# A sparse attention and gated feed-forward kernel: the first K through two cast loads, the row table early, one pair of the second chunk scored ahead

## The chip, the cores and the metric

The kernel runs on one core of a Trainium2 chip. A core has TensorE (PE: matmuls and their weight loads, PEld), VectorE (DVE), ScalarE (ACT), GpSimd (POOL) and SyncE (SP), each with its own queue of instructions that it works off in order, and 16 DMA engines that all queues share. DMAs are issued by SP, ACT and POOL; only those of POOL change the type on the way (a "cast load": float32 in memory, float16 in SBUF). The metric is the device time of the kernel in microseconds, the median of several runs. Matmul results land in PSUM, which has 8 banks.

## The reference

Block-sparse attention over 4 batches, 8 heads, 768 positions, head size 64, followed by a gated feed-forward layer on 3072 tokens:

```python
scores = (1/8) * q @ k^T                       # per batch and head, 768 x 768
mask = neighbours | first/last block row or column | sampled_blocks   # 32 x 32 blocks
attn = softmax(where(mask, scores, -1e9));  o = attn @ v
x = o transposed to (batch*seq, 512)
out = (sigmoid(x @ w_gate) * (x @ w_val)) @ w_out      # 512 -> 1536 -> 512, float32 out
```

The mask is the same for all batches and heads; three sampled blocks per block row come in as a table of 64-bit integers.

## The kernel before

The work is cut into 12 **chunks** n of 256 queries (three per batch) and, in each, 4 **pairs** p of heads. `attend(n, p, seq)` handles one pair of one chunk: three score tiles (TensorE, two banks each, L628), three exponentials on ScalarE (L646), values with the sum of the weights as a 65th column (L669), reciprocal and scaling on VectorE (L677, L680), and a transpose into x. For n = 0 the mask is added as a bias by extra matmuls in the scores (row table `e24`, called e in the trace, times `bias`); for every other chunk the exponentials are multiplied by a mask tile on VectorE (L654). Those nine mask tiles are made by `build_mask` (spread on TensorE L590, scaling on VectorE L598), and the bias by `expand` (L566, L575).

`ffn(g, seq)` handles the feed-forward of one chunk: 24 gate operations of 4 matmuls (L731, wg and wv in turn), a tanh on ScalarE (L750), a product on VectorE (L757), and 12 output operations of 2 matmuls (L775), then a scaling (L792) and a store.

Loads: the q, k and v of batch 0 come by POOL's cast loads (`load_half`, L429, in the order of FIRST); of pair 0, the first two sixths of q and k and the rest come apart. wg and wv (two halves each, L511) and w_out (three parts, L520) follow in the same queue. Later batches come as float32 by SP (`load`, L386), are cast by VectorE or ScalarE (`cast_qk`, `cast_v`) and, for q and k, transposed by DMA (`turn_dma`, L464). The q and k of batch 0 are transposed on TensorE (`turn_pe`, L447, copied out by L453).

The order is not written by hand. Each operation is handed to a `Plan` with an engine, an assumed duration, what it reads and writes, and a priority `prio` (lower is first). `Plan.run` plays a clock forward: whenever an engine is free it takes the operation of best priority whose inputs are there by the plan's own reckoning. The sequence that comes out is what each engine then executes in order. For loads the plan reckons a landing: a constant from LAND for the first ones, else a start after the issue (3.2 us for POOL, 1.9 for others), a shared DMA clock and `slack`. Operations `behind` others are only ordered after them. A value that is planned too early makes an engine wait in the program; it changes no result. While TensorE has nothing to do before 22 us of the plan, small matmuls on a zero tile (L370) are put in.

Rings hold the buffers: `pt` (exponentials, 12 tiles), x per pair and h per f (2 each). x limits how far attention runs ahead: the values of chunk n stand behind the last gate of chunk n - 2 (L834). From pair number CHAIN = 18 on, counted in order of scoring, a fixed sequence takes over TensorE: ROUND = "SoVgggoo", which is one pair's scores, an output operation, the values of the pair before, three times two gate operations, two output operations. Gates lag GLAG = 5 pairs behind and outputs OLAG = 9.

At the start, SP issues the small table mi, then q_in (early part of q, float32), k_in (later part of k, float32) and one half of e (L354); ACT issues the sampled blocks, ident, and the other half of e; POOL issues k_a (early part of k, cast), and then the list FIRST. ScalarE casts q_in (L483) and k_in (L484, giving k_b).

Of the kernel before, what the change touches and what calls it, by code (L numbers as in the profile page):

```python
# [9 lines left out]
f16 = mybir.dt.float16  # L10
f32 = mybir.dt.float32
# [4 lines left out]
B, H, S, D = 4, 8, 768, 64  # L16
BLK = 32
NB = S // BLK
NJ = S // 128
NP = H // 2  # L20
NCH = 3
CH = 256
# [5 lines left out]
VW = 66  # L28
SPIN = 22.0
NMASK = 1  # L30
FETCH = ((6, 1), (1, 2))
CHAIN, GLAG, OLAG, ROUND = 18, 5, 9, "SoVgggoo"
EDGES = [0, 768, 1536]
LAND = dict(sbi=2.9, mi=2.4, ident=3.1, e0=3.6, e1=3.9, q=2.9, kb=3.8, k=3.6)
FIRST = [
    ("k", 1), ("q", 1), ("k", 2), ("q", 2), ("v", 0), ("q", 0), ("k", 3), ("q", 3), ("v", 1), ("v", 2), ("v", 3),
]
HALF = [(0, 0), (0, 1), (0, 2), (0, 3)]
TURN_PE = 3
CAST_LATE = 12  # L40
GROUPS = [[i] for i in range(12)]
# [29 lines left out]
class Plan:  # L71
# [36 lines left out]
    def run(self):  # L108
# [10 lines left out]
        dma_free, mode, order, now = 0.0, None, [], 0.0  # L119
# [48 lines left out]
        while left:  # L168
            wake = []
            for e in LAT:  # L170
# [45 lines left out]
                o, where = best  # L216
# [7 lines left out]
                o.start, o.end = now, now + dur  # L224
                if o.lands is not None:
                    o.seen = o.lands
                elif o.dma:
                    first = now + (3.2 if e == "POOL" else 1.9)
                    if o.dma > 0.15:
                        first = dma_free = max(dma_free, first) + o.dma  # L230
                    o.seen = first + 0.3 + o.slack
                else:
                    o.seen = o.end + LAT[e]
# [13 lines left out]
            now = min(ahead)  # L247
# [13 lines left out]
def kernel(  # L261
# [11 lines left out]
    nc = tc.nc  # L273
# [40 lines left out]
    def psb(shape, dt=f32, homes=SINGLE, span=1):  # L314
        def make(i):
            t = psum[:, i : i + span].rearrange("p b c -> p (b c)")
            if dt != f32:
                t = t.bitcast(dt)
            n = int(np.prod(shape))
            t = t[:, 0:n]  # L320
            if len(shape) == 2:
                t = t.rearrange("p (a b) -> p a b", a=shape[0])
            return t

        b = Buf("ps", make)
        b.homes, b.span = homes, span
        return b

    def one(shape, dt, name):
        b = Buf(None, None)  # L330
        b.tile = sing.tile(shape, dt, name=name)
        return b
# [87 lines left out]
    def load_half(nm, b, p, prio, dur=0.72):  # L420
        cut = (nm, b, p) == ("q", 0, 0)
        js = later if cut else every
        if cut:
            c = one([128, 2, NJ - 2, 64], f16, "q16_late")
        else:
            c = sb(f"{nm}16" if nm != "v" else "vh", [128, 2, NJ, 64], f16)
        half16[nm, b, p] = stage[nm, b, p] = c
        o = P.op(
            "POOL", dur, lambda: nc.gpsimd.dma_start(c(), src[nm][b][:, 2 * p : 2 * p + 2, js]),  # L429
            writes=[c], prio=prio, dma=0.8 if cut else 1.0,  # L430
        )
        o.slack = 0.3 + b
        return o

    def turn_pe(nm, b, p, js, prio, behind=(), c=None, j0=0):
# [22 lines left out]
    def turn_dma(nm, b, p, prio):  # L458
# [6 lines left out]
            reads=[c], writes=[t], prio=prio, dma=1.3,  # L465
        )

    k_in, q_in = one([128, 2, NJ - 2, 64], f32, "k_in"), one([128, 2, 2, 64], f32, "q_in")
    k_a, k_b = one([128, 2, 2, 64], f16, "k16_a"), one([128, 2, NJ - 2, 64], f16, "k16_b")
    q_a = one([128, 2, 2, 64], f16, "q16_a")  # L470
    P.op(
# [1 line left out]
        lands=LAND["q"],  # L473
    )
    P.op(
        "SP", 0.5, lambda: nc.sync.dma_start(k_in(), src["k"][0][:, 0:2, later]), writes=[k_in], prio=-94, dma=1.0,
        lands=LAND["kb"],
    )
    P.op(
        "POOL", 0.82, lambda: nc.gpsimd.dma_start(k_a(), src["k"][0][:, 0:2, early]), writes=[k_a], prio=-95,  # L480
        dma=0.5, lands=LAND["k"],
    )
    P.op("ACT", 0.35, lambda: nc.scalar.copy(q_a(), q_in()), reads=[q_in], writes=[q_a], prio=-88)  # L483
# [100 lines left out]
    def build_mask(c, prio, behind):  # L584
# [21 lines left out]

    group_of = {n: (g, i) for g, ns in enumerate(GROUPS) for i, n in enumerate(ns)}
    xT = {
        (g, p): sb(f"x{p}", [128, 512], f16) for g in range(len(GROUPS)) for p in range(NP)
    }  # L610

    valued, scored = {}, []
# [1 line left out]
    def attend(n, p, seq):  # L614
# [3 lines left out]
        for tt in range(NCH):  # L618
# [25 lines left out]
            P.op(  # L644
                "ACT", 0.915,
                lambda st=st, pt=pt: nc.scalar.activation(  # L646
# [72 lines left out]
    def ffn(g, seq):  # L719
# [4 lines left out]
        for f in range(NF):  # L724
            both = psb([512])
            pair = [(both, 0), (both, 256)]
            for k, ((t, z), (nm, wt)) in enumerate(zip(pair, (("g", wg), ("v", wv)))):
# [15 lines left out]
                        behind=gates[-1:],  # L743
                    )
                )
            tg, h_ = sb("tg", [128, 512], f32), sb(f"h{f}", [128, 512], f16)
            hts[g, f] = h_
            P.op(
                "ACT", 0.17 + 0.43 * k_,
# [49 lines left out]
                )  # L799

    seq, turned, late_loads = 0, [], []
    for n in range(B * NCH):
        b, c = divmod(n, NCH)
        if n == 1:
            for p in range(NP):
                turn_pe("q", 0, p, later, 9.0, [valued[0, 1]], j0=2 if p == 0 else 0)
            expand(2, 4, 2, scored[1:2])
            build_mask(1, 11.5, scored[4:5])
            build_mask(2, 14.5, [valued[0, 2]])
            build_mask(0, 26, [valued[0, 3]])  # L810
        for p in range(NP):
            attend(n, p, seq)
            seq += 3
        if b + 1 < B:
            for p in range(NP) if c == 0 else ():
                if (b + 1, p) in HALF:
                    for nm in "kq":
                        turn_pe(nm, b + 1, p, every, 3 * NP * (3 * b + 2))
                    cast_v(b + 1, p, 3 * NP * (3 * b + 2))
                    continue  # L820
# [67 lines left out]
```

## Time and profile before

| | us |
|---|---|
| median of 6 runs | 292.85 (292.19 to 293.37) |
| the profiled execution | 292.73 |
| span from its first to its last instruction | 290.8 |
| TensorE busy in the span | 284.7 |
| ScalarE busy | 206.9 |
| VectorE busy | 196.3 |

Busy times are unions of the instructions' spans; matmuls are pipelined, so TensorE's busy time is not the time that its array computes. "Idle before" names what an engine waited for. TensorE's clock was granted in full all through. The DMA engines are loaded from 2 us to about 40 us, which is batch 0 and the weights, and less afterwards.

### The profile page before, as it was taken

To read this page: it belongs to the slowest core of one execution; us is meant where nothing else is said; L and a number is where in the kernel's file an instruction comes from. 1 tells how busy PE (TensorE), PEld (TensorE's weight loads), DVE (VectorE), ACT (ScalarE), POOL (GpSimd) and SP (SyncE) were. 2 spreads that over 40 slices of the span, in tenths; PEclk is the share of its full clock that TensorE was granted. 3 is DMA by queue.
4 is the path that set the end of the run, shared out by engine and by line. 5 is a ranking of instruction groups with operands and counts; after the bars stand their busy time and mean duration, and the time that the engine had idled before them with its cause. 6 is when DMAs were issued, how large, how long until landed. Compare 5 with 4: busy or idle time off the path is not lost.

```text
span 290.8 us, 8127 instructions
## 1 busy us (share of the span) xinstructions
PE 284.7 (98%) x3417; PEld 210.8 (72%) x3417; DVE 196.3 (67%) x458; ACT 206.9 (71%) x321; POOL 14.1 (5%) x23
## 2 busy tenths in 40 slices
PE   7999999999999999999999999999999999999995
PEld 6686766885786877777767767767777777777763
DVE  3479878997897577657867877756765765763230
ACT  3875589787988677678678678768768777772331
POOL 8730000000000000000000000000000000000000
PEclk9999999999999999999999999999999999999999
DMA  7999997991796873115477564011011020121003
GB/s 139 192 209 211 207 283 205 278 239 37 232 233 198 124 198 82 20 47 188 94 222 207 117 211 100 19 47 47 10 55 35 21 58 15 43 56 42 8 34 109
DMA packets 50788, 35.43 MB, mean 122 GB/s; under 512 B 31376, under 2 KB 47808, under 8 KB 50752
## 3 DMA queue, kind: packets, MB, share of 16 engines
q1 hardware_dynamic: 43576, 27.97, 36.9%
q0 software_dynamic: 6960, 6.88, 14.4%
q8 instruction: 26, 0.43, 0.7%
q14 instruction: 10, 0.08, 0.1%
q10 hardware_dynamic: 216, 0.07, 0.1%
HBM read 28.42 MB, written 6.29 MB: 119 GB/s over the span
## 4 chain that ended last, share of the span: by engine, by line
PE 90%; DMA 5%; POOL 3%; issue 1%; ACT 0%; POOLq 0%
PE psum L731 44%; PE psum L775 23%; PE psum L669 12%; PE psum L628 12%; DMA wv<-in_moe_w_val_dram 5%; POOL vh L429 1%; POOL q L429 1%; POOL k L429 1%; PE psum L590 0%; PE psum L705 0%; POOL k_a L480 0%; POOL wg L511 0%; POOL q_late L429 0%; ACT y L792 0%; POOLq L872 0%
## 5 line engine op out<-in xcount | busy, mean ns | idle before, releaser
L646 ACT ACTIVATE pt<-psum 128x1024 f16<-128x1024 f32 x144 | 138.9, 1026 | 23.6 <-PE psum L628 23.4
L654 DVE TENSOR_TENSOR pt<-pt,mask 128x1024 f16<-128x1024 f16 x132 | 89.3, 687 | 46.0 <-ACT pt L646 45.9
L731 PE MATMUL psum<-x,wv 128*128 128x256 f16 x576 | 86.5, 273 | 0.5 <-DMA wv<-in_moe_w_val_dram 0.5
L731 PE MATMUL psum<-x,wg 128*128 128x256 f16 x576 | 86.4, 272 | 0.0
L750 ACT ACTIVATE tg<-psum 128x256 f32<-128x256 f32 x144 | 56.0, 389 | 41.9 <-PE psum L731 40.0
L775 PE MATMUL psum<-wo,h 128*128 128x512 f16 (+1 forms) x300 | 75.4, 372 | 0.0
L757 DVE SCALAR_TENSOR_TENSOR h<-tg,psum 128x256 f16<-128x256 f32 x144 | 58.1, 416 | 24.1 <-ACT tg L750 23.5
L731 PEld LDWEIGHTS <-wv 128*128 128x128 f16 x576 | 55.4, 98 | 8.7 <-issue 1.7
L731 PEld LDWEIGHTS <-wg 128*128 128x128 f16 x576 | 53.5, 98 | 7.8 <-issue 1.3
L669 PEld LDWEIGHTS <-pt 128*128 128x128 f16 x1152 | 42.4, 97 | 9.6 <-issue 0.8
L628 PE MATMUL psum<-qT,kT 64*128 64x256 f16 x576 | 44.7, 271 | 0.0
L669 PE MATMUL psum<-v,pt 128*128 128x65 f16 x1152 | 44.3, 193 | 0.0
L775 PEld LDWEIGHTS <-h 128*128 128x128 f16 x300 | 26.1, 98 | 22.8 <-issue 7.6
L628 PEld LDWEIGHTS <-kT 64*128 64x128 f16 x576 | 24.4, 94 | 19.5 <-issue 16.7
L792 ACT ACTIVATE y<-psum 128x512 f32<-128x512 f32 (+1 forms) x22 | 12.7, 577 | 12.3 <-PE psum L775 12.3
L680 DVE TENSOR_TENSOR x<-psum,rz 128x256 f16<-128x256 f32 x48 | 20.3, 424 | 1.6
L677 DVE RECIPROCAL rz<-psum 128x4 f32<-128x4 f32 x48 | 8.6, 179 | 5.3 <-PE psum L669 5.1
L370 PE MATMUL psum<-zero 128*64 128x128 f16 x47 | 5.5, 277 | 1.0 <-DVE zero L340 1.0
L598 DVE TENSOR_SCALAR mask<-psum 128x512 f16<-128x512 f32 x9 | 6.1, 683 | 0.2
L628 PE MATMUL psum<-bias,e 64*128 64x256 f16 x48 | 5.8, 273 | 0.0
L406 DVE CAST v<-vs 128x768 f16<-128x768 f32 x10 | 5.5, 553 | 0.0
L370 PEld LDWEIGHTS <-zero 128*64 128x64 f16 x47 | 4.5, 147 | 1.4 <-DVE zero L340 1.0
(53 smaller groups left out, 69.9 us busy)
## 6 DMA issues: line engine op xcount, KB each, us to landing
out_dram<-y SPq DMA_DIRECT2D x23, 256.0 KB, 2.8
ks<-in_k_dram SPq DMA_DIRECT2D x12, 384.0 KB, 3.4
qs<-in_q_dram SPq DMA_DIRECT2D x12, 384.0 KB, 4.0
vs<-in_v_dram SPq DMA_DIRECT2D x12, 384.0 KB, 4.6
wg<-in_moe_w_gate_dram POOLq DMA_DIRECT2D x2, 768.0 KB, 13.5
wv<-in_moe_w_val_dram POOLq DMA_DIRECT2D x2, 768.0 KB, 16.4
wo<-in_moe_w_out_dram POOLq DMA_DIRECT2D x3, 512.0 KB, 21.8
vh<-in_v_dram POOLq DMA_DIRECT2D x4, 192.0 KB, 7.8
```

What stands on the lines that cost most here:

```text
L370: "PE", dur, lambda: nc.tensor.matmul(t()[0:64], zero()[:, 0:64], zero(), start=True, stop=True),
L429: "POOL", dur, lambda: nc.gpsimd.dma_start(c(), src[nm][b][:, 2 * p : 2 * p + 2, js]),
L628: nc.tensor.matmul(st()[:, hd, jj * CH : (jj + 1) * CH], l[r, 2 * tt + jj, :], m[r, 2 * c : 2 * c + 2, :], start=not (own and masked), sto ...
L646: lambda st=st, pt=pt: nc.scalar.activation(pt().rearrange("p h j q -> p h (j q)"), st(), AF.Exp, scale=SCALE),
L654: nc.vector.tensor_tensor(t, t, mask()[:, c, tt].unsqueeze(1).to_broadcast([128, 2, 512]), op=ALU.mult)
L669: nc.tensor.matmul(o()[:, 2 * jq + hd, 0:65], pts[j // 2]()[:, hd, j % 2, jq * 128 : jq * 128 + 128], v_[:, hd, j, 0:65], start=(j == 0), ...
L680: lambda: nc.vector.tensor_tensor(x16().rearrange("p j (h d) -> p (j h) d", d=64), o()[:, :, 0:64], rz().to_broadcast([128, 4, 64]), op=AL ...
L731: nc.tensor.matmul(t()[:, z : z + w], wt()[:, i, f * 128 : (f + 1) * 128], xT[g, i]()[:, 0:w], start=(i == 0), stop=(i == NP - 1),)
L750: lambda tg=tg, a=pair[0]: nc.scalar.activation(tg()[:, 0:w], a[0]()[:, a[1] : a[1] + w], AF.Tanh, scale=0.5),
L757: lambda tg=tg, a=pair[1], h_=h_: nc.vector.scalar_tensor_tensor(h_()[:, 0:w], tg()[:, 0:w], 1.0, a[0]()[:, a[1] : a[1] + w], op0=ALU.add, ...
L775: nc.tensor.matmul(py()[:, m], hts[g, f]()[:, tt * 128 : (tt + 1) * 128], wo()[:, f, m], start=(f == 0), stop=(f == NF - 1),)
L792: lambda py=py, y=y, m=m: nc.scalar.activation(y()[:, m], py()[:, m], AF.Copy, scale=0.5),
```

## The change

1. **First K.** k_in, its SP load and its ScalarE cast go. The later part of k of pair 0 comes as a second cast load on POOL, straight into k_b, right behind k_a.
2. **Row table early.** With k_in gone, SP issues its half of e right after q_in; on ACT, ident moves behind the other half of e (prio -98 to -92).
3. **Order of loads.** In FIRST, the later part of q of pair 0 moves from the sixth place to the first.
4. **Order of scoring.** EARLY = (0,0), (1,0), (0,1), (0,2), (0,3), then the rest as before. The transposes of the later part of q of pair 0, the second bias and masks 1 and 2 are ordered behind the first three score tiles, with new priorities; the other q transposes and mask 0 come when (1, 1) is reached. The rule that asks for two free double banks (`paired`) is left off for EARLY.
5. **Rings.** pt 12 to 15; x 2 to 4 (values of chunk n behind the gates of chunk n - 4); x, h and tg tiles are 256 wide instead of 512. CHAIN 18 to 16.
6. **The plan's reckoning.** New LAND constants; POOL loads start 2.5 us after issue instead of 3.2; slack of batch 0 0.3 to 0.4, of later batches 1.5 to 3.0, which orders the casts of these loads later; first loads on POOL count in the DMA clock.

```diff
+Q0P, M1P, M2P = -39.2, 14, 17
+XR, HR = 4, 2
+EARLY = [(0, 0), (1, 0), (0, 1), (0, 2), (0, 3)]
-CHAIN, GLAG, OLAG, ROUND = 18, 5, 9, "SoVgggoo"
+CHAIN, GLAG, OLAG, ROUND = 16, 5, 9, "SoVgggoo"
-LAND = dict(sbi=2.9, mi=2.4, ident=3.1, e0=3.6, e1=3.9, q=2.9, kb=3.8, k=3.6)
+LAND = dict(sbi=1.7, mi=1.6, ident=3.2, e0=3.4, e1=3.3, q=3.1, kb=4.4, k=3.5)
 FIRST = [
-    ("k", 1), ("q", 1), ("k", 2), ("q", 2), ("v", 0), ("q", 0), ("k", 3), ("q", 3), ("v", 1), ("v", 2), ("v", 3),
+    ("q", 0), ("k", 1), ("q", 1), ("k", 2), ("q", 2), ("v", 0), ("k", 3), ("q", 3), ("v", 1), ("v", 2), ("v", 3),
 ]
...
+                    dma_free = max(dma_free, o.lands - 0.3) if e == "POOL" else dma_free
-                    first = now + (3.2 if e == "POOL" else 1.9)
+                    first = now + (2.5 if e == "POOL" else 1.9)
...
-        ("v16", 8), ("vh", 4), ("pt", 12), ("rz", 2), ("x16", 4), ("tg", 2), ("y", 3),
+        ("v16", 8), ("vh", 4), ("pt", 15), ("rz", 2), ("x16", 4), ("tg", 2), ("y", 3),
...
-        P.ring(f"x{p}", 2)
+        P.ring(f"x{p}", XR)
-        P.ring(f"h{f}", 2)
+        P.ring(f"h{f}", HR)
...
-        "ACT", 0.4, lambda: nc.scalar.dma_start(ident16(), id_h.ap()), writes=[ident16], prio=-98, dma=0.1,
+        "ACT", 0.4, lambda: nc.scalar.dma_start(ident16(), id_h.ap()), writes=[ident16], prio=-92, dma=0.1,
...
-        o.slack = 0.3 + b
+        o.slack = 0.4 + 0.6 * b
...
-        "SP", 0.5, lambda: nc.sync.dma_start(k_in(), src["k"][0][:, 0:2, later]), writes=[k_in], prio=-94, dma=1.0,
+        "POOL", 0.72, lambda: nc.gpsimd.dma_start(k_b(), src["k"][0][:, 0:2, later]), writes=[k_b], prio=-94,
+        dma=0.8, lands=LAND["kb"],
-    P.op("ACT", 0.56, lambda: nc.scalar.copy(k_b(), k_in()), reads=[k_in], writes=[k_b], prio=-67)
...
-            o.paired, o.twin = not masked and 4 * n + p < CHAIN, psb([2, 512], homes=PAIR, span=2)
+            o.paired, o.twin = (n, p) not in EARLY and 4 * n + p < CHAIN, psb([2, 512], homes=PAIR, span=2)
...
+    order = EARLY + [i for i in order if i not in EARLY]
-        if n == 1:
+        if (n, p) == EARLY[1]:
+            turn_pe("q", 0, 0, later, Q0P, scored[:1], j0=2)
+            expand(2, 4, 2, scored[1:2])
+            build_mask(2, M2P, build_mask(1, M1P, scored[2:3]))
+        if (n, p) == (1, 1):
+            for i in range(1, NP):
+                turn_pe("q", 0, i, later, 9.0, [valued[0, 1]])
+            build_mask(0, 26, [valued[0, 3]])
-            for p in range(NP):
-                turn_pe("q", 0, p, later, 9.0, [valued[0, 1]], j0=2 if p == 0 else 0)
-            expand(2, 4, 2, scored[1:2])
-            build_mask(1, 11.5, scored[4:5])
-            build_mask(2, 14.5, [valued[0, 2]])
-            build_mask(0, 26, [valued[0, 3]])
...
-                    o.slack = 1.5
+                    o.slack = 3.0
...
-        g = group_of[n][0] - 2
+        g = group_of[n][0] - XR
```

More of the change, by code (lines that the diff above doesn't have):

```diff
@@ L466, in turn_dma @@
         )
-    k_in, q_in = one([128, 2, NJ - 2, 64], f32, "k_in"), one([128, 2, 2, 64], f32, "q_in")
+    q_in = one([128, 2, 2, 64], f32, "q_in")
     k_a, k_b = one([128, 2, 2, 64], f16, "k16_a"), one([128, 2, NJ - 2, 64], f16, "k16_b")
@@ L475 @@
     P.op(
[L476 to L479, printed above, removed]
         "POOL", 0.82, lambda: nc.gpsimd.dma_start(k_a(), src["k"][0][:, 0:2, early]), writes=[k_a], prio=-95,
@@ L482 @@
     )
+    P.op(
+        "POOL", 0.72, lambda: nc.gpsimd.dma_start(k_b(), src["k"][0][:, 0:2, later]), writes=[k_b], prio=-94,
+        dma=0.8, lands=LAND["kb"],
+    )
     P.op("ACT", 0.35, lambda: nc.scalar.copy(q_a(), q_in()), reads=[q_in], writes=[q_a], prio=-88)
-    P.op("ACT", 0.56, lambda: nc.scalar.copy(k_b(), k_in()), reads=[k_in], writes=[k_b], prio=-67)
     for i, (nm, p) in enumerate(FIRST):
@@ L608 @@
     xT = {
-        (g, p): sb(f"x{p}", [128, 512], f16) for g in range(len(GROUPS)) for p in range(NP)
+        (g, p): sb(f"x{p}", [128, CH * len(ns)], f16) for g, ns in enumerate(GROUPS) for p in range(NP)
     }
@@ L745, in ffn @@
                 )
-            tg, h_ = sb("tg", [128, 512], f32), sb(f"h{f}", [128, 512], f16)
+            tg, h_ = sb("tg", [128, w], f32), sb(f"h{f}", [128, w], f16)
             hts[g, f] = h_
@@ L801 @@
     seq, turned, late_loads = 0, [], []
-    for n in range(B * NCH):
+    order = [(n, p) for n in range(B * NCH) for p in range(NP)]
+    order = EARLY + [i for i in order if i not in EARLY]
+    for n, p in order:
         b, c = divmod(n, NCH)
-        if n == 1:
-            for p in range(NP):
-                turn_pe("q", 0, p, later, 9.0, [valued[0, 1]], j0=2 if p == 0 else 0)
-            expand(2, 4, 2, scored[1:2])
-            build_mask(1, 11.5, scored[4:5])
-            build_mask(2, 14.5, [valued[0, 2]])
-            build_mask(0, 26, [valued[0, 3]])
-        for p in range(NP):
[L812 to L820, printed above, removed]
+        if (n, p) == EARLY[1]:
[6 more added lines that the diff above has]
+            build_mask(0, 26, [valued[0, 3]])
+        attend(n, p, seq)
+        seq += 3
+        if p == NP - 1 and b + 1 < B and c == 0:
+            for p in range(NP):
                 for nm in "kqv":
```

## The prediction

> **What bounds the kernel now.** I read the page's busy shares first, then the chain of work that ended last, in order of time. In the page:
>
> ```profile
> PE 284.7 (98%) x3417; PEld 210.8 (72%) x3417; DVE 196.3 (67%) x458; ACT 206.9 (71%) x321; POOL 14.1 (5%) x23
> ```
>
> TensorE is the bound, and the chain shows how it runs once it is full:
>
> ```profile
> 103.47 2.62 PE psum L731 x24
> 106.09 0.86 PE psum L775 x4
> 106.95 0.76 PE psum L628 x12
> 108.25 0.76 PE psum L669 x24
> 109.01 2.62 PE psum L731 x24
> ```
>
> One round (24 gate matmuls, 6 output matmuls, one pair's scores and values) takes 109.01 - 103.47 = 5.54 us, without a stall, and repeats to 261 us. None of that work is touched. So the change can only win TensorE time lost in the filling, before both halves of wg and wv have landed. The second wv is issued at 13.13 and needs 19.3 us (its tile's view): 32.4 us. The timeline of that stretch:
>
> ```profile
> 1.80 0.46 SPq L476 DMA_DIRECT2D k_in<-in_k_dram  x1
> ...
> 2.30 0.43 SPq L354 DMA_DIRECT2D e<-bb_e  x1
> ...
> 6.10 0.30 PE L566 MATMUL psum<-e,mb 128*64 128x256 f16 x2 [0.89 <-DMA e<-bb_e]
> ...
> 6.92 0.28 PE L628 MATMUL psum<-bias,e 64*128 64x256 f16 x2
> ...
> 7.57 2.85 ACT L646 ACTIVATE pt<-psum 128x1024 f16<-128x1024 f32 x3 [1.89 <-PE psum L628]
> ...
> 24.92 0.61 PE L731 MATMUL psum<-x,wv 128*128 128x256 f16 x4 [0.49 <-DMA wv<-in_moe_w_val_dram]
> ```
>
> The first score waits for the bias, the bias for the table e, and e's SP half is issued behind the 256 KB of k_in. All else follows from that first exponential. The same stretch in windows, columns PE, PEld, DVE, ACT and POOL busy, clock, DMA share, GB/s:
>
> ```profile
> 7.57:20.70 13.13, 12.73 (x258) 9.64 (x258) 7.25 (x21) 11.53 (x12) 7.58 (x11) 1.00 1.25 200
> 20.70:24.92 4.22, 3.73 (x55) 2.43 (x52) 3.98 (x11) 1.95 (x2) 0.00 (x0) 1.00 1.16 209
> 24.92:32.40 7.48, 7.48 (x84) 5.43 (x84) 6.79 (x15) 4.64 (x9) 0.00 (x0) 1.00 1.17 209
> ```
>
> To 20.70, ACT is the feeder: 12 exponentials (the four pairs of chunk 0) in 13.13 us, 1.60 idle. VectorE is idle for 13.13 - 7.25 = 5.9 us there and then full (3.98 of 4.22, 6.79 of 7.48), because all nine mask tiles (L598, 683 ns each) are built only then. In 20.70 to 24.92 ACT manages 2 exponentials. That imbalance is what the change works on.
>
> How much has TensorE lost there? Between its first score (6.92) and 32.4 lie 25.5 us. Useful at their own pitch: 12 masked score tiles x 0.43, 5 plain x 0.22, 5 value groups x 0.79, 80 transposes x 0.03, 10 of x x 0.055, 8 mask spreads x 0.24, 11 gates x 0.44: 19.8. So 5.7 us is loss, and some 2.5 of it (a dozen changes between scores and full matmuls, each an "issue" gap of 0.21 on PEld) stays. The ceiling is about 3.2 us plus what an earlier start gives.
>
> **The change, part by part.**
>
> *K by two cast loads, e earlier.* Removed: SP's k_in (256 KB) and ACT's cast of it (0.62 us at 5.07). Added: one POOL issue of 128 KB, 0.72 us by the L429 rows, second in POOL's queue. e's SP issue moves from 2.30 to 1.80, its ACT issue from 1.80 to 1.37; ident goes behind it, 1.37 to 1.80, and at its 2.3 us lands at 4.1, under the q_a cast that ends at 4.32: no cost. With nothing large in front, e should land like the neighbouring small loads (ident 2.3 us, q_in 2.7 us after issue): 4.1 to 4.5, not 6.07. From e's landing to the first score took 6.92 - 6.07 = 0.85; but VectorE must then also copy the first kT and qT (0.29 each), which before were done ahead of the bias. k_a lands at 1.23 + 3.2 = 4.43, transposes and copies to 5.3. I take the first score at 5.6 (5.2 to 6.3): **1.3 us earlier**, and ACT with it (6.25).
>
> Is k_b in time for the second score tile? Here a rule speaks against the change: the Trainium skill, DMA: Bandwidth & Descriptors, sections Specifications and Issuing engine by pattern, calls the sync/scalar path generally faster, with a first byte after about 0.6 us against 1 us from GpSimd. The rows: k_in on SP took 3.2 us for 256 KB; k_a on POOL took 3.2 us for 64 KB; the POOL load now in k_b's place, k of pair 1 (192 KB), took 4.9. By the page's difference alone k_b would land 0.4 later than its bytes ask, about 1.80 + 3.2 + 0.25 + 0.4 = 5.6 (estimate); by the row of the same place 2.05 + 4.9 = 6.95, less about 0.3 for 64 KB fewer, 6.6. Without k_in in the engines beside it I take 5.4. k_in plus its cast was ready at 5.69, so at 5.4 nothing is lost, and at 6.6 the second exponential starts at 7.9 instead of 7.2: 0.7 of the 1.3 gone, still no loss against 8.5 before.
>
> *Queue positions.* Every later POOL load is issued 0.72 us later, and q_late moves ahead of k of pair 1. POOL waits for landings from 9.5 on (for k of pair 2, then q of pair 2) and wg is issued at 10.49 but lands at 21.2, so issue is not what limits; bytes are. The same skill page (Queues, rings and completion order) says each DMA engine takes turns between its queues packet by packet: bytes moved from SP's queue to POOL's then cost the weights nothing. The rows allow a little: the DMA share is 0.87 and 1.12 in 2:4 and 4:6 against 1.28 after, so bytes moved out of the early stretch may not find their place; 128 KB at 200 GB/s is 0.65 at most. I take weights 0.2 later; TensorE has attention meanwhile, so 0.1 on the end. q of pair 1 lands some 0.5 later than 7.95, but is now wanted only after the six tiles of pair 0, near 11: hidden.
>
> *Chunk 1 of pair 0 scored second.* Its transposes (8), VectorE copy (0.42), three plain tiles and values come forward, needing only q_late (about 6.2). It fills ACT while pairs 1 and 2 land: the 1.60 idle goes. 1.3 + 1.6 = 2.9 us of ACT, three exponentials at 0.95: all of (1, 0) is through by 20.7. Masks 1 and 2 are built from the third score on, six in the 5.9 us that VectorE has idle (6 x 0.69 = 4.1).
> TensorE work pulled ahead of 20.7: three tiles x 0.25 + values 0.79 + six spreads x 0.24 = **3.0 us**.
>
> *Refill.* That work is then missing between 20.7 and 32.4. Gates can't replace it (f 6 to 11 need the halves landing at 28.6 and 32.4). Further tiles can: VectorE, freed of six masks (4.1 us), can take 4.1 / 0.98 = 4 tiles more (0.69 multiply, 0.29 share of normalising), ACT too (6.6 of 11.7 busy). They bring 4 x 0.51 = 2.0, plus 0.25 of mode change each where they come singly. I count 2.2 of the 3.0 kept.
>
> *Rings (pt 15, x 4) and CHAIN 16.* pt lets a fifth pair be in flight, which (1, 0) needs; x 4 lets chunk 2's values go before group 0's gates; half-width tiles move nothing. Part of the refill, no extra. Two more rounds in the written order: TensorE has no gap in the chain from 83 to 95, and its rounds there, less regular, are no slower than 5.54 by more than the 0.2 of one mode change: 0.5 either way, I take 0.
> *Later casts ordered later* (slack 1.5 to 3.0): the page has no wait of DVE or ACT on a batch load, so nothing to win; batch 1's kT is issued at 45.87 and wanted near 60 (the 30 exponentials before 50.0 are all of batch 0, which has 36), so 1.5 us later is hidden; without that cover it costs 1.5.
>
> **Sum** against the profiled execution's 292.73 (span 290.8 + 1.9 around it): 2.2 - 0.1 = 2.1 less, 290.6; it stands 0.12 under the median 292.85, so **290.7**.
>
> **The rivals.**
> *More is won* (refill complete, chunk 1 fed without gaps): the ceiling, 3.2 + 0.4: about 289.2. For it: VectorE and ACT have the room. Against: singly scored tiles cost a mode change each.
> *Spent again*: the early work is done, and TensorE then waits at 24.9 and 32.4 for weights, which the change doesn't hasten: 292.5. For it: the wait at 24.92. Against: attention tiles are ready for such holes.
> *Slower: the order written for TensorE puts a transpose ahead of ready scores while its load is still out.* The plan now assumes POOL loads 0.7 us sooner after issue (2.5 for 3.2), with only 0.1 more slack in batch 0. Before, one such place cost 0.65 (PEld for q of pair 3 at 14.59). Behind it stand all scores, and ACT behind these. If seven K/Q loads each held it 0.6, that is 4.2, against 2.9 of ACT time won: 1.3 lost, 294.0. It decides from 0.4 us per load upwards; below that the two or three tiles waiting in PSUM hide it.
>
> **How the numbers follow.** Gain as summed 0.50; more 0.17; spent 0.15; slower 0.18. The measurement tells about 0.2% (0.6 us) from no change. The first two are faster, "spent" mostly within: faster 0.70, same 0.12, slower 0.18. The likeliest case alone spans 289.6 to 291.9 (k_b at 6.6, weights 0.65 late, refill 1.2 to 3.0). To leave out 2 in 10, the range reaches to 289.0 below and through half of the slower case above: 293.9.
>
> **What would show it.** Right: no wait for e at L566, first score near 5.6, no ACT cast of k_b; 15 exponentials by 20.7; L598 begun before 20; L731 first at 24 to 25; then the same 5.54 us rounds, 2 us earlier. Wrong: waits of PE for DMA k or q in 6 to 16; DVE full before 20 with ACT waiting for it; gaps at L731 between 24 and 33.

## The result and the profile after

The changed kernel takes 292.32 us (median of 33 runs, 291.20 to 293.37) against 293.3 for the kernel before in the same comparisons: a ratio of 0.996 (0.9949 to 0.997), or 1.0 us less between the medians (1.2 by the ratio). The forecast was 2.1 us less. The profiled execution took 292.0 us, with a span of 290.2. In the listings of after, the scores are L631, the exponentials L649, the mask multiply L657, the values L672, the gates L734, the outputs L778, the transposes of q and k L451.

TensorE is still the bound:

```profile
PE 283.3 (98%) x3410; PEld 211.0 (73%) x3410; DVE 192.3 (66%) x448; ACT 211.4 (73%) x330; POOL 14.9 (5%) x24
```

The chain of waits of after once TensorE is full (start, length, what; "x24" counts matmuls):

```profile
91.71 2.62 PE psum L734 x24
94.33 0.86 PE psum L778 x4
95.19 0.76 PE psum L631 x12
95.96 0.54 PE psum L778 x2
96.49 0.77 PE psum L672 x24
97.26 2.62 PE psum L734 x24
```

The round is 97.26 - 91.71 = 5.55 us, as before. The filling, in the timeline of after (start, length, engine and line, shapes, and in brackets the idle time before and what ended it):

```profile
4.61 0.30 PE L569 MATMUL psum<-e,mb 128*64 128x256 f16 x2 [0.64 <-DMA e<-bb_e]
...
5.87 0.41 PE L451 MATMUL psum<-ident,k_b 128*64 128x128 f16 x8 [0.49 <-DMA k_b<-in_k_dram]
...
6.33 0.28 PE L631 MATMUL psum<-bias,e 64*128 64x256 f16 x2
...
6.98 8.72 ACT L649 ACTIVATE pt<-psum 128x1024 f16<-128x1024 f32 x9 [1.55 <-PE psum L631]
...
9.99 0.30 PE L451 MATMUL psum<-ident,q 128*64 128x128 f16 x4 [0.45 <-DMA q<-in_q_dram]
...
14.56 0.53 PE L451 MATMUL psum<-ident,k 128*64 128x128 f16 x12 [0.65 <-DMA k<-in_k_dram]
15.02 0.94 PE L672 MATMUL psum<-v,pt 128*128 128x65 f16 x24
...
28.56 0.61 PE L734 MATMUL psum<-x,wg 128*128 128x256 f16 x4
```

The row table e is there 1.46 us earlier (4.61 for 6.07), but the written order puts the transposes of k_b ahead of the first score, and k_b landed at 5.82: the first score starts at 6.33, 0.6 us earlier than before, and the first exponential at 6.98 (7.57). Later TensorE waits for q of pair 1 and for k of pair 3, and in order behind the latter stand the first values. They start at 15.02 (12.29 before) and the first gate at 28.56 (23.82). The same stretches in windows of after, up to 20.70 (columns as in the windows of before: PE, PEld, DVE, ACT and POOL busy, clock, DMA share, GB/s):

```profile
6.98:20.70 13.72, 12.58 (x245) 9.11 (x246) 10.14 (x25) 11.52 (x12) 8.94 (x13) 1.00 1.23 190
20.70:24.92 4.22, 4.22 (x68) 2.88 (x69) 3.56 (x11) 3.51 (x4) 0.00 (x0) 1.00 1.16 210
24.92:32.40 7.48, 6.92 (x105) 5.48 (x105) 7.28 (x17) 6.52 (x9) 0.00 (x0) 1.00 1.16 210
```

ScalarE did 12 exponentials by 20.7, exactly as many as before (x12 in both rows); three more had been forecast. Its idle time there went up from 1.60 to 13.72 - 11.52 = 2.20 us.

**Where the microsecond came from.** I counted the matmuls that TensorE had begun by several marks and gave each the price it has in the steady round (a score matmul 0.063 us, values 0.0325, gate 0.109, output 0.2165):

| us of that work done by | 20.7 | 32.4 | 70 | 80 | 95 | 110 |
|---|---|---|---|---|---|---|
| before | 5.40 | 12.98 | 48.20 | 57.55 | 71.79 | 86.64 |
| after | 5.36 | 12.62 | 48.00 | 57.75 | 72.57 | 87.29 |
| difference | -0.04 | -0.36 | -0.20 | +0.20 | +0.78 | +0.65 |

The table leaves out the matmuls of bias, mask spreads and transposes. By 32.4 after has done one mask spread (0.24 us) and two transposes more, about 0.3 us, so the -0.36 there is nearly even. The filling, which the change is about, brought nothing: even at 32.4, 0.2 us behind at 70. These are single executions. Two other kernels that execute after's sequence up to 46 us (CHAIN 18 and slack 1.5, below) stand at 12.62 and 13.28 by 32.4, so a few tenths there mean little. The gain arises between 70 and 95 us, where the diff touches nothing but the order. Here is that stretch in the chain of before, with every stretch of scores in it and a few of its neighbours:

```profile
70.96 0.76 PE psum L669 x24
71.73 0.43 PE psum L775 x2
72.16 0.54 PE psum L628 x8
...
74.10 0.54 PE psum L628 x8
74.64 0.54 PE psum L775 x2
75.18 0.77 PE psum L669 x24
75.95 0.54 PE psum L628 x8
...
79.10 0.54 PE psum L628 x8
...
82.81 0.33 PE psum L628 x4
...
84.87 0.54 PE psum L628 x8
...
89.02 0.54 PE psum L628 x8
...
91.74 0.33 PE psum L628 x4
...
92.60 0.54 PE psum L628 x8
```

And all scores between 70 and 95 us in the chain of after, with what lies between the last two:

```profile
71.59 0.76 PE psum L631 x12
...
75.81 0.54 PE psum L631 x8
...
77.33 0.54 PE psum L631 x8
77.88 0.54 PE psum L778 x2
78.42 0.76 PE psum L672 x24
79.18 9.61 PE psum L734 x88
88.78 0.86 PE psum L778 x4
89.65 0.76 PE psum L631 x12
```

These lines hold a price. Four scores take 0.33, eight 0.54, twelve 0.76: 0.215 for each four, and 0.11 for entering a stretch of scores (scores that follow each other with no other matmul between). Leaving it costs as much: two outputs take 0.43 behind values and 0.54 behind scores. So each stretch of scores costs 0.22 us above its own matmuls. A score matmul uses 64 rows of the array, as a mask spread does; gates, outputs and values use 128 (`64*128` and `128*128` in the timeline's lines). The Trainium skill (TensorEngine Tiling (Array Packing), Key Properties) says that a change of tiling mode drains TensorE, which fits; the trace shows the price, not the drain. Before has nine stretches between 70 and 95 us, after four; over the whole trace, mask spreads counted in, it is 66 against 61. Five fewer at 0.22 are 1.1 us. The table, with the 0.3 us that it leaves out, shows about 0.7 gained from 32.4 to 110 us, and the two profiled executions differ by 292.73 - 292.0 = 0.73: the right size, and some 0.4 too much. One agreement is no proof; the runs on CHAIN and slack below put it to the test.

### The profile page after: what moved, and what is told of

It is laid out like the page before. It is cut to its first block, busy times and chain, and to the rows that moved or that the text cites. A ratio compares the mean times of both kernels' runs of the same rounds, so it can differ in the third digit from the quotient of the medians.

```text
span 290.2 us, 8113 instructions
## 1 busy us (share of the span) xinstructions
PE 283.3 (98%) x3410; PEld 211.0 (73%) x3410; DVE 192.3 (66%) x448; ACT 211.4 (73%) x330; POOL 14.9 (5%) x24
## 4 chain that ended last, share of the span: by engine, by line
PE 93%; DMA 3%; POOL 2%; DVE 1%; issue 0%; ACT 0%; POOLq 0%
PE psum L734 44%; PE psum L778 23%; PE psum L672 13%; PE psum L631 12%; DMA k<-in_k_dram 3%; PE psum L708 1%; PE psum L451 1%; POOL k L433 0%; POOL q L433 0%; PE psum L593 0%; POOL k_a L480 0%; POOL q_late L433 0%; POOL k_b L484 0%; POOL vh L433 0%; DVE mask L601 0%
## 5 line engine op out<-in xcount | busy, mean ns | idle before, releaser
L649 ACT ACTIVATE pt<-psum 128x1024 f16<-128x1024 f32 x144 | 138.4, 1027 | 20.6 <-PE psum L631 20.3
L657 DVE TENSOR_TENSOR pt<-pt,mask 128x1024 f16<-128x1024 f16 x132 | 89.1, 687 | 50.0 <-ACT pt L649 49.9
L734 PE MATMUL psum<-x,wv 128*128 128x256 f16 x576 | 86.4, 273 | 0.0
L734 PE MATMUL psum<-x,wg 128*128 128x256 f16 x576 | 86.3, 272 | 0.0
L778 PE MATMUL psum<-wo,h 128*128 128x512 f16 (+1 forms) x300 | 75.1, 372 | 0.0
L734 PEld LDWEIGHTS <-wv 128*128 128x128 f16 x576 | 55.9, 98 | 7.0 <-issue 0.6
L734 PEld LDWEIGHTS <-wg 128*128 128x128 f16 x576 | 53.5, 98 | 7.4 <-issue 0.6
L672 PEld LDWEIGHTS <-pt 128*128 128x128 f16 x1152 | 42.4, 98 | 9.4 <-issue 0.8
L631 PE MATMUL psum<-qT,kT 64*128 64x256 f16 x576 | 44.4, 271 | 0.2 <-DVE x L713 0.2
L672 PE MATMUL psum<-v,pt 128*128 128x65 f16 x1152 | 44.5, 193 | 0.0
L778 PEld LDWEIGHTS <-h 128*128 128x128 f16 x300 | 26.2, 98 | 23.1 <-issue 7.4
L631 PEld LDWEIGHTS <-kT 64*128 64x128 f16 x576 | 24.6, 94 | 19.5 <-issue 15.9
L795 ACT ACTIVATE y<-psum 128x512 f32<-128x512 f32 (+1 forms) x24 | 13.9, 579 | 13.0 <-PE psum L778 13.0
L631 PE MATMUL psum<-bias,e 64*128 64x256 f16 x48 | 6.2, 273 | 0.0
L421 ACT CAST q<-qs 128x768 f16<-128x768 f32 x7 | 5.9, 849 | 0.0
L374 PEld LDWEIGHTS <-zero 128*64 128x64 f16 x40 | 3.9, 152 | 1.7 <-DVE zero L344 1.0
```

The lines of the kernel that those rows point to most:

```text
L374: "PE", dur, lambda: nc.tensor.matmul(t()[0:64], zero()[:, 0:64], zero(), start=True, stop=True),
L631: nc.tensor.matmul(st()[:, hd, jj * CH : (jj + 1) * CH], l[r, 2 * tt + jj, :], m[r, 2 * c : 2 * c + 2, :], start=not (own and masked), sto ...
L649: lambda st=st, pt=pt: nc.scalar.activation(pt().rearrange("p h j q -> p h (j q)"), st(), AF.Exp, scale=SCALE),
L657: nc.vector.tensor_tensor(t, t, mask()[:, c, tt].unsqueeze(1).to_broadcast([128, 2, 512]), op=ALU.mult)
L672: nc.tensor.matmul(o()[:, 2 * jq + hd, 0:65], pts[j // 2]()[:, hd, j % 2, jq * 128 : jq * 128 + 128], v_[:, hd, j, 0:65], start=(j == 0), ...
L734: nc.tensor.matmul(t()[:, z : z + w], wt()[:, i, f * 128 : (f + 1) * 128], xT[g, i]()[:, 0:w], start=(i == 0), stop=(i == NP - 1),)
```

## The experiments

The ratio given is to the kernel before, with its 95% interval; the change itself stands at 0.996. "Order kept" means that every engine executes the sequence that after has, so only what is named differs. Elsewhere the plan makes a new order.

### Is the filling held by K on GpSimd's queue, by the order of scoring, or by the weights?

**K by SP behind e, order kept.** k_b comes through a float32 load on SP and ScalarE's cast again, but behind e:

```diff
-        "POOL", 0.72, lambda: nc.gpsimd.dma_start(k_b(), src["k"][0][:, 0:2, later]), writes=[k_b], prio=-94,
+        "POOL", 0.72, lambda: nc.sync.dma_start(k_in(), src["k"][0][:, 0:2, later]), writes=[k_b], prio=-94,
...
+            if c is k_b:
+                nc.scalar.copy(k_b(), k_in())
```

> The changed kernel with every engine's written order kept, but the later part of K comes again as float32 by SP (behind its half of e) and is cast by ScalarE just before its transposes. Theory 'queue' (the second cast load puts every later cast load and the weights 1.1 to 1.9 us back, and that ate the gain): q of pair 1 and k of pair 3 land about 1 us earlier than 9.94 and 14.52, both waits of TensorE (0.45, 0.65) go, wv lands near 25.0; about 0.8 us faster than the changed kernel, ratio to the kernel before 0.993. Theory 'order' (scoring (1, 0) second puts the values of (0, 3), and with them the first gate at 28.56, too late, whatever the loads do): the first gate moves by 0.3 at most, ratio 0.996 as in the changed kernel.

Measured 1.0043 (1.0028 to 1.0059). Both expected ratios missed. The landings did come sooner, as the first theory had it (q of pair 1 at 9.41 for 9.94, k of pair 3 at 13.52 for 14.52, the first half of wv at 25.14 for 25.96), so the second cast load does hold up that queue. But the timeline of this kernel shows a load of K that landed far later than before:

```profile
2.27 0.39 SPq L486 DMA_DIRECT2D k_in<-in_k_dram  x1
...
7.38 0.62 ACT L450 CAST k_b<-k_in 128x512 f16<-128x512 f32 x1 [1.74 <-DMA k_in<-in_k_dram]
...
8.05 0.41 PE L453 MATMUL psum<-ident,k_b 128*64 128x128 f16 x8 [2.15 <-ACT k_b L450]
```

Before, k_in was issued at 1.80 and landed at 5.04; issued 0.47 us later, it landed 2.3 us later. The first score moves 2.18 us (8.51), the first gate 2.18 (30.74), the span 2.1: with the order kept, this late start is found again at the end. TensorE's clock also fell in this stretch (last section), so the two are not separated.

**Natural order of scoring**, planned anew:

```diff
-EARLY = [(0, 0), (1, 0), (0, 1), (0, 2), (0, 3)]
+EARLY = [(0, 0), (0, 1), (0, 2), (0, 3), (1, 0)]
```

> The changed kernel with EARLY in natural order, (0,0) (0,1) (0,2) (0,3) (1,0): everything else, loads too, as changed; the plan writes its order anew. Theory 'order': the values of (0, 3) run by 22, the first gate at wv's landing near 26, and the time is about 0.7 us below the changed kernel, ratio 0.9935. Theory 'queue': ScalarE waits again for pairs 1 to 3 early on, the gain of the early pair is gone, ratio 0.999 to 1.002.

Measured 1.002 (1.0003 to 1.0036). The first gate comes at 25.69, nearly 3 us sooner than in after, and the kernel is slower all the same: ScalarE then stands idle while K and Q of pairs 1 and 2 land (2.16 us before 11.94 alone). So scoring (1, 0) second does fill ScalarE early on, as the prediction had it, and the late first gate is no measure of loss. The order behind 32 us is another one here too, so the loss isn't shown to come from the filling alone.

**The weights later, order kept**: one more cast load of 192 KB in front of wg, into a tile that nobody reads, and the same in the kernel before.

```diff
+                if (nm, a) == ("g", 0):
+                    nc.gpsimd.dma_start(spare(), src["v"][0][:, 0:2])
```

> The changed kernel, order kept, with one unused cast load of 192 KB issued ahead of wg: wg and wv land about 1 us later than in the changed kernel (wv's first half near 27.0). Theory 'queue': the weights' landing bounds, so 0.5 to 1.0 us slower than the changed kernel, ratio 0.998 to 0.999. Theory 'order': the first gate waits for x of (0, 3), written at 27.9, not for the weights: no difference, ratio 0.996.

> The kernel before, order kept, with one unused cast load of 192 KB ahead of wg: wg and wv about 1 us later. If the kernel before is bound by the weights (its first gate pair waits for wv at 24.92), 0.5 to 1.0 us slower: ratio 1.002 to 1.0035. If not: 1.000.

Measured 0.995 (0.9935 to 0.9966) on after and 1.0018 (1.0004 to 1.0032) on before. In after the first half of wv now lands at 27.65 for 25.96, and nothing comes of it; in before the same load costs 0.5 us. The weights held the kernel before in part, and don't hold after.

**K by SP behind e, with the plan told its landings** (CHAIN 17, earlier mask 1), and **K on SP ahead of e as before, with (1, 0) scored second** (CHAIN 14):

> A candidate: the changed kernel with the later part of K by SP and ScalarE behind e, the plan told the landings that the two traces show, CHAIN 17, mask 1 at priority 9. Both theories: no waits of TensorE on loads between 6 and 16 and weights at 24.9. Theory 'queue': about 1 us below the changed kernel, ratio 0.9925. Theory 'order': values of (0, 3) still near 24, first gate near 27 to 28, ratio 0.996.

> The changed kernel with the first K as in the kernel before (SP, ahead of e, cast by ScalarE), so e is late again, but with (1, 0) scored second and the plan told the landings that fit this. If the early pair carries the gain alone: 0.9925 to 0.995, like the candidate with K on POOL (0.9926). If the early start through e is needed as well: first score near 7, ratio 0.997 to 0.999.

Measured 1.0014 (0.9994 to 1.0033) and 1.0009 (0.9992 to 1.0025). Both missed. In the first, k_in landed at 7.13, 4.86 us after its issue; the plan had been told 4.48 on its own clock. In the second k of pair 1 held TensorE for 1.15 us at 8.42. Neither way of loading K by SP beats the cast load.

### Which wait holds the filling of after?

**First score ahead of k_b's transposes**, the rest of the order kept:

```diff
+        first = next(o for o in order if o.fn.__name__ == "scores")
+        turn = next(o for o in order if o.prio == -40 and o.eng == "PE")
+        order.remove(first)
+        order.insert(order.index(turn), first)
```

> The changed kernel, order kept but for one thing: the first score tile stands ahead of k_b's transposes on TensorE (in the changed kernel it was ready at about 5.6 and stood behind them until 6.33). As the prediction has it (an earlier first exponential is an earlier end): 0.6 us below the changed kernel, ratio 0.994. Theory 'held by one load': first score near 5.7, first exponential near 6.3, but TensorE only waits longer for k of pair 3 at 14.5; no difference at the end, ratio 0.996.

Measured 0.9963 (0.9949 to 0.9977), no different from the change. The first score starts at 5.68, what the prediction had hoped for. The timeline of this kernel shows where it went:

```profile
14.82 0.53 PE L455 MATMUL psum<-ident,k 128*64 128x128 f16 x12 [1.20 <-DMA k<-in_k_dram]
15.28 0.93 PE L676 MATMUL psum<-v,pt 128*128 128x65 f16 x24
```

The wait for k of pair 3 is longer by 0.55 (1.20 for 0.65). The head start of 0.65 us is spent there.

**One load fewer**, order kept: the later part of q of pair 0 is filled with zeros by GpSimd and not loaded (its scores are therefore not the reference's).

```diff
-            "POOL", dur, lambda: nc.gpsimd.dma_start(c(), src[nm][b][:, 2 * p : 2 * p + 2, js]),
+            "POOL", dur, lambda: nc.gpsimd.memset(c(), 0.0) if cut else nc.gpsimd.dma_start(c(), src[nm][b][:, 2 * p : 2 * p + 2, js]),
```

> The changed kernel, order kept, with the later part of q of pair 0 not loaded at all (GpSimd fills the tile with zeros, so the output is not the reference's): every POOL load behind it and the weights have 128 KB less ahead of them. Theory 'held by one load' (the written order puts the transposes of k of pair 3 in front of the values of pair 0 and of ready scores of pair 2, so its landing at 14.52 and nothing before it sets what follows): k of pair 3 lands near 13.9, the wait of 0.65 goes, all later work and the end come 0.6 earlier, ratio to the kernel before 0.994 (the changed kernel has 0.996). Theory 'order of pairs alone' (only the place of (0, 3) counts): 0.996.

Measured 0.9926 (0.9899 to 0.9952), 1.0 us below the change, whose interval it only just touches. Its timeline:

```profile
13.36 0.57 PE L451 MATMUL psum<-ident,k 128*64 128x128 f16 x12
...
27.68 0.61 PE L734 MATMUL psum<-x,wg 128*128 128x256 f16 x4
```

No wait for k of pair 3 (landed at 13.27 for 14.52), and the first gate 0.88 sooner. The loads between came 0.6 to 0.9 sooner as well, and the wait for q of pair 1 fell from 0.45 to 0.2, so this run alone doesn't isolate one load. With the run before it, it points to the landing of k of pair 3 as what sets the filling in after's order; the start and the weights don't.

### Can the plan be given the true landings?

**Only k of pair 3's landing told**; **all landings told**, CHAIN 14, masks at 13 and 15; and **the same in natural order**, CHAIN 15, masks at 12 and 15:

```diff
+SEEN = {'k3': 13.8}
...
-            writes=[c], prio=prio, dma=0.8 if cut else 1.0,
+            writes=[c], prio=prio, dma=0.8 if cut else 1.0, lands=SEEN.get(f"{nm}{p}"),
```

> The changed kernel with one number told truly: the plan takes k of pair 3 to land at 14.52 of the trace instead of 1.7 us sooner; the plan then writes everything behind it anew. If a truer landing makes a better order by itself: 0.5 to 1.0 us below the changed kernel, ratio 0.993. If the written order is decided by how the greedy plan happens to fall, a truer number is no better: its values of pair 1 and of (0, 3) come later in the plan than before, ratio 0.999 to 1.002.

> A candidate: the changed kernel, same loads and same order of scoring, but the plan is told the landings that the trace of the changed kernel shows (k_b 5.8, k of pair 1 8.6, k of pair 3 14.5, wv 26.0 and so on, with small offsets), CHAIN 14, masks at 13 and 15. Theory 'held by one load': the first scores go before the transposes of k_b, k of pair 3 goes behind ready scores; 0.8 to 1.3 us below the changed kernel, ratio 0.992. Theory 'order of pairs alone': values of (0, 3) stay near 24, ratio 0.996.

> As the candidate with the measured landings, but with the pairs in natural order, (1, 0) last of the five; CHAIN 15, masks at 12 and 15. If scoring (1, 0) second is itself the gain: slower than the kernel before, ratio 1.002 as in the run with natural order and the unchanged plan. If what counts is that the written order agrees with the landings, and that order of pairs matters little: ratio 0.994 to 0.996.

Measured 1.0026 (1.0005 to 1.0047), 0.9926 (0.9897 to 0.9955) and 0.9984 (0.9969 to 0.9999); the last lies between its two expectations. The first shows how little a better number guarantees: the wait at 14.56 is gone, and the kernel is 1.9 us slower than after, because the plan takes whatever is ready first and one changed landing makes it write another order (first gate 29.45). The second is the best that I ran, 291.34 us, and beats the kernel before; its interval just overlaps that of the change. Its one profile fell on its slowest execution (292.51), so where its gain lies is open; the wait for k of pair 3 isn't in it.

### Does the gain come from the parts that the prediction had put at nothing?

CHAIN, the slack of the later batches' casts and the rings, taken back in after, together and one by one (pt and x count as one), and then put alone into the kernel before:

```diff
-XR, HR = 4, 2
+XR, HR = 2, 2
-CHAIN, GLAG, OLAG, ROUND = 16, 5, 9, "SoVgggoo"
+CHAIN, GLAG, OLAG, ROUND = 18, 5, 9, "SoVgggoo"
...
-        ("v16", 8), ("vh", 4), ("pt", 15), ("rz", 2), ("x16", 4), ("tg", 2), ("y", 3),
+        ("v16", 8), ("vh", 4), ("pt", 12), ("rz", 2), ("x16", 4), ("tg", 2), ("y", 3),
...
-                    o.slack = 3.0
+                    o.slack = 1.5
```

> The changed kernel with the rings and the tail as before: pt 12, x 2, CHAIN 18, slack of later loads 1.5. Predicted cost of this part 0 (0.5 either way): ratio 0.994 to 0.998. If the rings carry the gain (values of chunk 2 ahead of the gates of chunk 0): ratio near 1.000.

> The changed kernel with CHAIN 18 as before, all else as changed. New theory 'fewer mode changes': the filling gained nothing (TensorE had done as much by 60 us in the kernel before), the gain comes from 60 to 110 us, where TensorE goes to scores and back 9 times instead of 13, at 0.2 us each; CHAIN 18 brings 4 of the changes back (2 stretches), so 0.4 slower than the changed kernel, ratio 0.9975. If the filling carries the gain: 0.996.

> The changed kernel with slack 1.5 for later batches as before, all else as changed. Theory 'fewer mode changes': two stretches more, 0.4 slower, ratio 0.9975. If late casts or transposes bind (the run with all of this part undone showed TensorE waiting 0.94 and 1.2 for kT and qT of batch 1): waits of TensorE for kT or qT near 64, 1 us slower, ratio 0.9995. As predicted (hidden either way): 0.996.

> The changed kernel with the rings as before (x 2, pt 12), CHAIN 16 and slack 3.0 kept. Theory 'fewer mode changes': one stretch of scores more, 0.2 slower, ratio 0.9965. If the rings carry the gain (attention may run two chunks further ahead): 0.999.

> The kernel before with this part alone: pt 15, x 4, half-wide tiles, CHAIN 16, slack 3.0; loads, K, order of pairs and the plan's landings as before. Theory 'fewer mode changes', if the parts add: 0.6 to 1.0 below the kernel before, ratio 0.997. If the parts don't add, since the plan writes the whole order anew for each: its own reckoning ends 2.7 us later than that of the kernel before, ratio up to 1.009.

| | ratio | interval | stretches of scores and mask spreads in its trace |
|---|---|---|---|
| after | 0.996 | 0.9949 to 0.997 | 61 |
| all of it back | 0.9992 | 0.9974 to 1.001 | 63 |
| CHAIN 18 | 0.9978 | 0.9969 to 0.9987 | 63 |
| slack 1.5 | 0.9984 | 0.9969 to 1.0 | 63 |
| rings | 0.9961 | 0.9947 to 0.9976 | 62 |
| alone, in before | 1.0038 | 1.0011 to 1.0064 | 63 (before: 66) |

With all of it back, the whole gain is gone, though the new loads, the early row table and the early pair are all still there. CHAIN and slack carry about 0.5 us (0.18%) and 0.7 us (0.24%); the rings carry nothing. The intervals of CHAIN 18 and slack 1.5 just reach that of the change. Two stretches more at 0.22 are 0.44 us, near both.

For CHAIN the traces bear this out. The kernel with CHAIN 18 executes after's sequence up to 76.2 us; then it has three more stretches by 95 us and two more by 110, and by the measure of the table above it stands at 72.14 and 86.96, 0.43 and 0.33 behind after. TensorE, VectorE and ScalarE wait for no load between 32 and 110 us in either.

For slack a second cause remains. TensorE waits for no load between 32 and 110 us with slack 1.5 either, but VectorE does (us in total, times, longest):

```profile
DVE q L419 <- DMA qs<-in_q_dram: 1.1, 1, 1.1
DVE k L419 <- DMA ks<-in_k_dram: 0.8, 1, 0.8
DVE v L410 <- DMA vs<-in_v_dram: 0.4, 1, 0.4
```

ScalarE waits 0.9 for v as well. Neither before nor after has such a wait there, so slack 3.0 does keep these casts from standing in the way. In the traced execution TensorE lost only 0.08 us to the last of them (busy for 2.42 of the 2.50 us from 60 to 62.5), but that was the fastest of this kernel's 14. How the 0.7 us divides between late casts and stretches is open. Where all is back, the waits are longer (VectorE 5.2 us, ScalarE 2.2), and one for a load reaches TensorE, in its timeline:

```profile
63.68 0.39 PE L631 MATMUL psum<-qT,kT 64*128 64x256 f16 x4 [0.94 <-DMA qT<-q]
```

It is part of that run's loss; the trace is of its slowest execution (294.79, median 293.39).

Put into the kernel before, the same three parts lose 1.1 us, although they take three stretches out there too. The chain of that kernel has pieces that neither before nor after has in these 25 us:

```profile
72.05 1.03 ACT pt L646
...
85.10 0.61 ACT pt L646
...
86.02 1.03 ACT pt L646
```

TensorE waits for exponentials: it is busy for 23.68 of the 25 us between 70 and 95, where before and after have 25.00. The fixed rounds begin earlier (88.8) with no more scores done beforehand than before: 34 score tiles by 60 us, as many as before, against 40 in after. So the early pair has a use after all, if not the one forecast: it lets attention run ahead (22 tiles by 32.4 us, for 17), and with that stock the earlier rounds find their exponentials ready. That the stock makes the difference is read from these traces and was not varied by itself.

## Why the prediction was right and wrong

**Sign and range** held (0.996, forecast 0.993), but by luck: the mechanism did not. The sum was 2.2 for the filling and 0.1 back for the weights, with nothing for rings, CHAIN and later casts. The term of 2.2 failed, and under it the step on queue positions (below). The filling brought about nothing (even with before at 32.4 us): the loads behind K came 1.7 to 2.0 us later, the written order waited for them, and 12 exponentials were done by 20.7, as before, not 15. One load taken out of that queue wins 1.0 us back; the rest of the 2.2 isn't traced to one cause. The whole gain lies in the later part, through CHAIN (0.5) and slack (0.7), which were put at nothing.

**First score 1.3 us earlier: half.** e came 1.46 earlier, with SP's queue shorter. On ScalarE nothing moved: in spite of its new priority, ident was still issued ahead of e (1.37 and 1.80, as before). The bias and its copies were ready about 5.6. But the written order has k_b's transposes first, so the landing of k_b counted for the first score, not for the second: 5.82, against 5.4 taken, 5.6 worked out with the Trainium skill's first-byte figures (DMA: Bandwidth & Descriptors, Specifications) and 6.6 by the row of the same queue place. The kernel that scores first shows that the missing half is worth nothing in this order.

**Queue positions: the step that failed.** It said that issue doesn't limit the loads on GpSimd, that q of pair 1 comes 0.5 later, and that this is hidden until near 11. Two more issues of 0.72 us stand ahead of k of pair 1 (issued at 3.46 for 2.04), and it landed 1.70 later; q of pair 1, k and q of pair 2 and k of pair 3 each landed 1.7 to 2.0 later. TensorE stood waiting for q of pair 1 from 9.54. Issue isn't all of it: k of pair 3 was issued only 0.70 later. Nor were the bytes neutral. The windows of before and then of after:

```profile
4.00:7.00 3.00, 1.82 (x30) 1.44 (x31) 1.07 (x4) 0.93 (x2) 3.00 (x5) 1.00 1.21 195
7.00:12.00 5.00, 5.00 (x90) 3.62 (x92) 2.25 (x6) 4.19 (x5) 4.23 (x7) 1.00 1.26 185
```

```profile
4.00:7.00 3.00, 1.90 (x34) 1.49 (x34) 1.05 (x3) 0.73 (x3) 3.00 (x5) 1.00 1.09 135
7.00:12.00 5.00, 4.51 (x78) 2.90 (x79) 2.84 (x6) 4.85 (x6) 4.38 (x7) 1.00 1.20 161
```

From 4 to 12 us before moves 3 x 195 + 5 x 185 = 1510 KB, after 3 x 135 + 5 x 161 = 1210 KB: 300 KB less. Up to 128 KB of that is only counting, as the cast load counts 128 KB where k_in counted 256; at least 170 KB, 0.9 us at 200 GB/s, were left for later. GpSimd is busy issuing all through 4 to 7 in both; what SP had brought beside it in the same time now has to queue. With K back on SP and the order kept, k of pair 3 landed 1.0 sooner again. The upper bound of 0.65 us for the weights was the wrong size too: the halves of wv land 1.1 and 1.6 later. It cost nothing only because the order of after asks for the weights later as well (the run with the weights later still).

**Chunk 1 second, three exponentials more by 20.7: refuted.** It fills ScalarE at the start (nine exponentials without a gap from 6.98 to 15.70), but gaps of 1.08, 0.24 and 1.30 us follow, the first of them behind k of pair 3.

**Refill, 2.2 of 3.0: not reached.** There was nothing pulled ahead by 20.7 to keep (5.36 us of work done for 5.40; beside that, three mask spreads more and ten bias matmuls fewer). Masks were built earlier: VectorE works 10.1 us from the first exponential to 20.7, for 7.25. Tiles of later chunks did fill the stretch to 32.4 (22 score tiles for 17), but in place of gates (5.5 groups of four for 11), not beyond them.

**The slower rival** described what happened in the filling: transposes of loads that are still out stand ahead of ready scores. Three loads held TensorE (0.49, 0.45, 0.65 us), not seven, and the runs point to the largest as the one on the path.

**Rings and CHAIN, 0 with 0.5 either way; later casts, 0.** Rings: right. CHAIN: 0.5, at the end of its bound; put into before together with slack and rings, where no stock of scores stands behind it, a loss. Slack: 0.7. The prediction saw no wait of VectorE or ScalarE for a batch load in before and concluded that there was nothing to win; it asked neither whether such waits come up in the new order, as they do with slack 1.5, nor what other order the plan writes when it thinks the batch comes later. The prediction counted "a dozen changes between scores and full matmuls" in the filling and allowed the two added rounds one of 0.2 each; that the rounds could gather the scores into fewer stretches (four in after for nine) it did not see.

## What to carry to other kernels

Where a planner writes the order, an edit to a due time, a ring or a landing is an edit to the whole order: compare the two orders along the whole path that binds, above all the number of switches between matmuls of different array use (0.22 us for each excursion here), before pricing the edit by its own place. A load moved to another queue delays what stands behind it there (here by 1.7 to 2.0 us for loads of 192 KB, with 0.72 us of issue for each load put ahead). And an earlier start is worth only what the next late landing leaves of it.

## What the hardware showed unexpectedly

TensorE's granted clock fell in the run with K on SP, after the 2.15 us wait at 8.05. Its windows:

```profile
7.00:12.00 5.00, 3.95 (x45) 2.23 (x47) 0.85 (x2) 2.83 (x4) 3.82 (x7) 0.72 1.25 184
12.00:16.00 4.00, 4.00 (x68) 2.72 (x65) 3.20 (x7) 3.63 (x5) 3.05 (x5) 0.93 1.31 203
```

Pairs of score matmuls at 9.41 to 9.84 follow each other at 0.21 us where they took 0.11 at 8.51 to 8.84. The Trainium skill (TensorE: Matmul & The Clock Gate, Part 1) speaks of an idle window of about 3.4 us before the clock is halved; here 2.15 us without matmuls, between stretches with few, was enough. In the traces of before and after, the same windows show 1.00.

The kernel before has such a fall in some executions too: of the 55 beside the run with slack 1.5, 14 have a mean granted clock of 0.992 to 0.994 and a median of 293.91 us, the other 41 of 293.33. None of after's 33 is below 0.998. At full clock the two kernels still lie 1.0 us apart, so this isn't the gain. It is part of what the runs with K on SP lose: 6 of the 20 with the order kept and 7 of the 22 in each of the others had a mean clock of 0.988 to 0.994, and medians 0.6 to 2.1 us above the rest of the same kernel.

The other surprise is k_in on SP: 256 KB took 3.24 us issued at 1.80, and 5.09 us issued at 2.27, behind both halves of e and two of GpSimd's loads in place of one. That the competition with those loads is the cause is likely, and wasn't isolated. How much single landings vary from execution to execution also stays open: k of pair 3 was seen from 13.8 to 15.2 us over the kernels that share after's first loads.
